# Decays over a whole tile of 128 positions, mirrored features folded in one step, and another order of attention, transpose and background steps

## The chip, the core and the metric

One NeuronCore of a Trainium2 chip runs the whole program. The metric is the time of one execution on the device, in microseconds (us); the median of three runs of the kernel before is 634.03 us (633.94 to 634.5). The change is small against that, so a verdict needs several runs of both kernels.

## What is computed

```python
# gated linear attention, batch 4, 8 heads, 768 positions, head size 48
for t in range(S):
    state = alpha[:, :, t, :, None] * state + einsum('bhd,bhe->bhde', k[:, :, t], v[:, :, t])
    y[:, :, t] = einsum('bhd,bhde->bhe', q[:, :, t], state)
x = y with the heads side by side            # (4, 768, 384)
u = x + real(fft(fft(x, axis=1), axis=2))    # over positions, then over features
un = (u - mean(u)) / sqrt(var(u) + 1e-6)
x2 = u + relu(un @ w_ch1) @ w_ch2            # 384 -> 1536 -> 384
out = (sigmoid(conv5(x2)) * (x2 @ w_val)) @ w_out
```

## The kernel before, in words

All matmuls are in fp32 or in pairs of fp32r halves (three matmuls stand for one product). The work is cut in three ways: the attention runs over tiles of 128 positions (6 tiles for each of the 4 batches, numbered g), the Fourier part over a batch, and the rest (norm, 384 to 1536 to 384, gate) over pieces of 256 positions, 12 in all. The weights arrive as 64-bit floats, and VectorE makes fp32 of them with three instructions of bit operations for each block of 384 columns (L222, L225, L229; `weight_parts`, and `convert_one` later on), ScalarE makes the high half (L233) and the low half comes from TensorE and ScalarE (L242 to L244) or from VectorE (L238).

**One attention tile** has four steps. `attn_a` makes running products of the decays with two scans (L288 from behind, L295 from the front, each restarted at a segment's end by a column of `ends` or `starts`), and multiplies k and q with them (L293, L298). Segments are 64 positions long, so a tile has two chunks and its scans have 8 segments of 65 columns. `attn_b` transposes k (L310), copies it (L311), and makes the scores chunk by chunk (L318), which VectorE masks (L319). `attn_c` makes the chunks' outer products of k and v (L335) and then steps the state twice: `sp` = state times the chunk's decay (L346), state = product + `sp` (L351). `attn_d` puts the scores times v (L366) and q times `sp` (L372) together, and copies the result to `x` with three ScalarE copies (L377 to L379) and one column by GpSimd (L380): features 1 to 255, feature 0 again, and the features from 383 down to 256, so that each feature and its mirror image (d and 384 - d) stand in two runs that are walked in step.

**The Fourier part** of a batch transposes `x` (`turn`, L472), adds and subtracts tiles t and t + 3 (L483, L484 in `fold`), and then adds and subtracts each feature and its mirror image: for each of two halves and two signs one instruction over 128 columns (L490) and one over 64 that reads backwards (L491), so eight for each of three t. GpSimd copies one column (L488). Matmuls follow (L514, L559), and the sums go into `u` (L564 to L583).

**The order of the work** is written by hand. Up to the first piece a list of strings, `FIRST`, gives it letter by letter: A, B, D the attention's steps, U and S the two parts of `attn_c`, w a part of a weight conversion, l weight loads, a, v, q loads of one tile, 0 to 2 `turn`, f, g, h `fold`, p and r matmuls of the Fourier part. From then on `run` walks through the matmuls of a piece (`mlp`, 24 parts); after each part it advances the norm of the next piece and the gate of the last one (`side`), the weight conversions, and a background generator that does attention and Fourier part of the next batch (`attention` by the string `ORDER`, in which a dot ends a part). How many background parts come after a part of `mlp` follows from `PACE`. The norm makes its reciprocal root on GpSimd (L630 to L636), writes it to DRAM (L640) and loads it back as rows (L644); `LAG_US`, `LAG_SS` and `LAG_RS` say how many parts it waits between its steps. All loads and stores go through SyncE's queue in program order; among them is the convolution's small weight table, `cw`, converted like the others.

In the text below S(b, i) is the state step (L346 and L351) of tile i of batch b, S(i) that of batch 0, and A, B, D, U likewise.

Of the kernel before, what the change touches and what calls it, by code (L numbers as in the profile page):

```python
# [33 lines left out]
CHECK_STEP = 5  # L34
# [15 lines left out]
W_DFT = (2, 1, 1, 0, 0, 0, 0, 0, 0, 1, 0)  # L50
# [10 lines left out]
A_W = 1 + 8 * (C + 1)  # L61
# [3 lines left out]
class Main:  # L65
# [21 lines left out]
    def constants(self):  # L87
# [11 lines left out]
        nc.vector.memset(self.ends.rearrange("p (g s) -> p g s", s=C + 1)[:, :, C : C + 1], 1.0)  # L99
# [176 lines left out]
    def attn_a(self, g):  # L276
# [189 lines left out]
    def turn(self, b, t):  # L466

        nc = self.nc
        for i in (t, t + 3):
# [701 lines left out]
```

## Time and profile before

The profiled execution took 632.62 us; its span, from the first to the last instruction, is 630.5 us. Times below are from the span's start.

| engine | busy us | share of the span | instructions |
|---|---|---|---|
| PE (matmul) | 584.1 | 93% | 6636 |
| PEld (weight load) | 547.1 | 87% | 6636 |
| DVE (VectorE) | 427.8 | 68% | 953 |
| ACT (ScalarE) | 242.7 | 38% | 577 |
| POOL (GpSimd) | 155.3 | 25% | 331 |

PE is near its limit over the span, but a mean says nothing of where the rest lies: the first matmul of the first piece (L651) stands at 88.09 us, and the stretches before and shortly after it look different from the rest.

### The profile page before, as it was taken

The page shows a single profiled execution, that of the slowest core. Times are in us where ns is not written, and L with a number is a line of the kernel's source. Part 1 is how long each engine was busy: PE and PEld are TensorE (multiplying, and loading weights), DVE is VectorE, ACT ScalarE, POOL GpSimd, SP SyncE. Part 2 cuts the span into 40 slices and gives each one's busy share as a digit, 9 for nine tenths or more (in the row PEclk, how much of TensorE's full clock was granted, in tenths as well). Part 3 has the DMA queues.
Part 4 walks back from the last instruction along what each step waited for, and adds up shares of the span by engine and source line. Part 5 has one row for each costly group of instructions (what it writes and reads, how often), then busy time and mean ns, then how long its engine had stood idle before and what let it go on. Part 6 is the DMA issues. An engine that isn't in the chain of part 4 may idle for free.

```text
span 630.5 us, 15960 instructions
## 1 busy us (share of the span) xinstructions
PE 584.1 (93%) x6636; PEld 547.1 (87%) x6636; DVE 427.8 (68%) x953; ACT 242.7 (38%) x577; POOL 155.3 (25%) x331
## 2 busy tenths in 40 slices
PE   3768899697999999999999999999999999999996
PEld 2546768686998899989999899899999999999995
DVE  7988779899926567966673858967763726363634
ACT  2333442224454355344453343353453344423222
POOL 0000215104125122133131144232312222322230
PEclk9868998789899999999999999999999999999998
DMA  9746352646232446633424433642431023110001
GB/s 350 276 139 232 110 175 10 190 151 153 73 119 74 101 133 147 152 115 91 122 78 98 124 107 73 196 132 85 115 107 37 26 80 82 52 10 26 9 3 55
DMA packets 29602, 69.50 MB, mean 110 GB/s; under 512 B 5200, under 2 KB 15952, under 8 KB 29520
## 3 DMA queue, kind: packets, MB, share of 16 engines
q1 hardware_dynamic: 29520, 68.38, 37.1%
q8 instruction: 54, 0.88, 0.6%
q14 instruction: 28, 0.23, 0.1%
HBM read 63.64 MB, written 4.73 MB: 108 GB/s over the span
## 4 chain that ended last, share of the span: by engine, by line
PE 70%; DVE 19%; DMA 4%; POOL 2%; issue 2%; ACT 2%; SPq 1%; DVEq 0%; POOLq 0%
PE ch L651 7%; PE mm L651 7%; PE ch L653 7%; PE ch L652 7%; PE mm L653 6%; PE mm L652 6%; PE aux L762 5%; PE aux L514 4%; PE aux L559 3%; PE aux L318 3%; DVE w L295 2%; DVE w L288 2%; PE aux L651 2%; PE aux L653 2%; PE aux L652 2%
## 5 line engine op out<-in xcount | busy, mean ns | idle before, releaser
L651 PE MATMUL ch<-hh,w2h 128*128 128x256 f32 x432 | 130.2, 301 | 0.2 <-ACT hh L672 0.2
L651 PE MATMUL mm<-hl,w1h 128*128 128x256 f32 x432 | 129.0, 298 | 1.0 <-ACT hl L608 1.0
L653 PE MATMUL ch<-hlo,w2h 128*128 128x256 f32 x432 | 122.9, 285 | 1.5 <-DVE hlo L674 1.5
L652 PE MATMUL ch<-hh,w2l 128*128 128x256 f32 x432 | 122.8, 284 | 0.0
L653 PE MATMUL mm<-hl,w1h 128*128 128x256 f32 x432 | 121.9, 282 | 0.0
L652 PE MATMUL mm<-hl,w1l 128*128 128x256 f32 x432 | 121.8, 282 | 0.0
L674 DVE SCALAR_TENSOR_TENSOR hlo<-mm,hh 128x512 fp32r<-128x512 f32 x72 | 49.5, 688 | 85.8 <-ACT hh L672 85.7
L651 PEld LDWEIGHTS mm<-hl,w1h 128*128 128x128 f32 x432 | 82.3, 190 | 4.0 <-ACT hl L608 1.4
L651 PEld LDWEIGHTS ch<-hh,w2h 128*128 128x128 f32 x432 | 82.5, 191 | 2.7 <-ACT hh L672 0.4
L653 PEld LDWEIGHTS ch<-hlo,w2h 128*128 128x128 f32 x432 | 82.8, 192 | 1.9 <-DVE hlo L674 1.9
L652 PEld LDWEIGHTS ch<-hh,w2l 128*128 128x128 f32 x432 | 82.7, 192 | 0.8
L652 PEld LDWEIGHTS mm<-hl,w1l 128*128 128x128 f32 x432 | 82.4, 191 | 0.8
L653 PEld LDWEIGHTS mm<-hl,w1h 128*128 128x128 f32 x432 | 82.4, 191 | 0.3 <-DVE hl L611 0.3
L672 ACT ACTIVATE hh<-mm 128x512 fp32r<-128x512 f32 x72 | 42.6, 591 | 59.7 <-PE mm L653 59.5
L726 DVE SCALAR_TENSOR_TENSOR ga<-u,cw,ga 128x256 f32<-128x256 f32 x132 | 58.0, 501 | 0.0
L748 POOL TENSOR_TENSOR hl<-ga,hl 128x256 fp32r<-128x256 f32 x33 | 25.6, 780 | 96.5 <-ACT hl L747 96.5
L617 POOL TENSOR_TENSOR tmp<-tmp,tmp 128x256 f32<-128x256 f32 x24 | 20.3, 847 | 100.6 <-ACT tmp L616 99.7
L380 POOL COPY x<-x 128x1 f32<-128x1 f32 x24 | 12.9, 535 | 123.3 <-ACT x L377 123.3
L318 PEld LDWEIGHTS aux<-w 48*64 48x64 f32 x768 | 27.5, 149 | 16.1 <-issue 8.2
L318 PE MATMUL aux<-w 48*64 48x64 f32 x768 | 30.8, 236 | 11.1 <-DVE w L298 6.0
L762 PE MATMUL aux<-wvo,hl 128*128 128x384 f32 x180 | 34.9, 337 | 0.0
L607 DVE TENSOR_TENSOR w<-u,aux 128x256 f32<-128x256 f32 x36 | 13.0, 417 | 28.2 <-PE aux L601 27.5
(182 smaller groups left out, 1184.2 us busy)
## 6 DMA issues: line engine op xcount, KB each, us to landing
qka<-in_qka_dram SPq DMA_DIRECT2D x23, 772.5 KB, 5.2
ck<-in_w_dram SPq DMA_DIRECT2D x24, 384.0 KB, 3.4
vu<-in_vu_dram SPq DMA_DIRECT2D x24, 192.0 KB, 3.6
u<-in_w_dram SPq DMA_DIRECT2D x12, 384.0 KB, 6.1
va<-in_va_dram SPq DMA_DIRECT2D x24, 192.0 KB, 4.0
ck<-in_al_dram SPq DMA_DIRECT2D x12, 384.0 KB, 3.4
out_dram<-ga SPq DMA_DIRECT2D x22, 192.0 KB, 1.9
w<-in_cs_dram SPq DMA_DIRECT2D x6, 579.0 KB, 5.2
```

The lines of the kernel that those rows point to most:

```text
L318: nc.tensor.matmul(out=sc[j * 64 : j * 64 + 64, cs], lhsT=kt[hs, cs], rhs=qt[hs, cs], start=True, stop=True)
L514: self.nc.tensor.matmul(out=pa[: d1 - d0, g * 193 : g * 193 + n], lhsT=self.eo[g][:, t, m, d0:d1], rhs=self.cs[g][:, t, m, :n], start=t == ...
L559: nc.tensor.matmul(out=pa[:, :385], lhsT=self.cd[:w, dt, mi, kt * P : (kt + 1) * P], rhs=pq[:w, mi, dt, :], start=dt == 0, stop=dt == 1)
L617: nc.gpsimd.tensor_tensor(out=ss, in0=ss, in1=sq, op=ALU.add)
L651: nc.tensor.matmul(out=out, lhsT=w[0][:, k, cols], rhs=xh, start=first, stop=False)
L652: nc.tensor.matmul(out=out, lhsT=w[1][:, k, cols], rhs=xh, start=False, stop=False)
L653: nc.tensor.matmul(out=out, lhsT=w[0][:, k, cols], rhs=xl, start=False, stop=last)
L672: nc.scalar.activation(out=hh, in_=hp, func=AF.Relu)
L674: nc.vector.scalar_tensor_tensor(out=hl, in0=hp, scalar=0.0, in1=hh.bitcast(F32), op0=ALU.max, op1=ALU.subtract)
L726: nc.vector.scalar_tensor_tensor(out=gs[:, j], in0=xs, scalar=w, in1=gs[:, j], op0=ALU.mult, op1=ALU.add)
L748: nc.gpsimd.tensor_tensor(out=gl[:, j], in0=gs[:, j], in1=gh[:, j].bitcast(F32), op=ALU.subtract)
L762: nc.tensor.matmul(out=po[:, :DM], lhsT=lh[:, k, ts], rhs=rh[:, k, :], start=n == 0, stop=n == 8)
```

## The change

Segments of the scans are now a whole tile: 4 segments of 129 columns. The decay of the second chunk is then part of q and k already, so the state is multiplied once for a tile: `s0` = state times the tile's decay, `s1` = `s0` + first product, state = `s1` + second product. For the first tile of a batch it is a copy and an addition, for the last one a multiplication and an addition. `x` is 386 columns wide; a feature and its mirror image now stand side by side, so `attn_d` writes it with two ScalarE copies that leave every second column out, and `fold` needs one instruction over 191 columns for each half and sign, which reads every second column twice. `turn` transposes columns 2, 4, ..., then 258 to 385, then 3, 5, .... The bound below which a decay sends the program to its general path goes from 0.5 to 0.6. `FIRST`, `ORDER`, `PACE` and `W_DFT` are other tables, `LAG_US` and `LAG_SS` go from 6 to 5, `CHECK_STEP` from 5 to 6.

```diff
-LAG_US = 6
-LAG_SS = 6
+LAG_US = 5
+LAG_SS = 5
-ORDER = "Bb.Aa..Dt.m.Cvc.q."
+ORDER = ".BAab..Dt..mCvc.q."
...
-A_W = 1 + 8 * (C + 1)
+A_W = 1 + NP * (P + 1)
...
@@ attn_c
-        pe = r["pend"].rearrange("p (a c) -> p a c", c=2)
         r["sp"] = self.t([P, 2, NP, D], "sp", 2)
-        for c in range(2):
-            if g % NT == 0 and c == 0:
-                st = self.t([P, NP, D], "st", 2)
-                nc.vector.tensor_copy(out=st, in_=ub[c])
-            else:
-                sp = r["sp"][:, c]
-                nc.vector.tensor_tensor(out=sp, in0=self.state,
-                                        in1=pe[:, :, c : c + 1].to_broadcast([P, NP, D]), op=ALU.mult)
-                if last and c == 1:
-                    break
-                st = self.t([P, NP, D], "st", 2)
-                nc.vector.tensor_tensor(out=st, in0=ub[c], in1=sp, op=ALU.add)
-            self.state = st
+        s0, s1 = r["sp"][:, 0], r["sp"][:, 1]
+        if g % NT == 0:
+            nc.vector.tensor_copy(out=s1, in_=ub[0])
+        else:
+            nc.vector.tensor_tensor(out=s0, in0=self.state, in1=r["pend"].unsqueeze(2).to_broadcast([P, NP, D]),
+                                    op=ALU.mult)
+            nc.vector.tensor_tensor(out=s1, in0=ub[0], in1=s0, op=ALU.add)
+        if not last:
+            self.state = self.t([P, NP, D], "st", 2)
+            nc.vector.tensor_tensor(out=self.state, in0=ub[1], in1=s1, op=ALU.add)
@@ attn_d
-        nc.scalar.activation(out=xt[:, :n], in_=yp[0][:, :n], func=AF.Copy)
-        nc.scalar.activation(out=xt[:, n:256], in_=yp[1][:, : 256 - n], func=AF.Copy)
-        nc.scalar.activation(out=xt[:, 257:385], in_=yp[1][:, n - 1 : 255 - n : -1], func=AF.Copy)
-        nc.gpsimd.tensor_copy(out=xt[:, 256:257], in_=xt[:, 0:1])
+        nc.scalar.activation(out=xt[:, 0:DM:2], in_=yp[0][:, :n], func=AF.Copy)
+        nc.scalar.activation(out=xt[:, DM + 1 : 1 : -2], in_=yp[1][:, :n], func=AF.Copy)
+        nc.gpsimd.tensor_copy(out=xt[:, 1 : DM + 1 : DM - 1], in_=xt[:, 0:1].to_broadcast([P, 2]))
@@ turn
-            for j in range(KD):
-                nc.tensor.transpose(pa[:, j * P : (j + 1) * P], self.x[:, i, j * P + 1 : (j + 1) * P + 1], self.ident)
+            x = self.x[:, i]
+            for j, xj in enumerate((x[:, 2:258:2], x[:, 258:], x[:, 3:258:2])):
+                nc.tensor.transpose(pa[:, j * P : (j + 1) * P], xj, self.ident)
@@ fold
-            nc.gpsimd.tensor_copy(out=e[:, 0, 0:1], in_=f[:, 0:1])
+            nc.gpsimd.tensor_copy(out=e[:, 0, ::192], in_=f[:, :: DM + 1])
             for m, o2 in ((0, ALU.add), (1, ALU.subtract)):
-                nc.vector.tensor_tensor(out=e[:, m, 1:129], in0=f[:, 1:129], in1=f[:, 257:385], op=o2)
-                nc.vector.tensor_tensor(out=e[:, m, 129:193], in0=f[:, 129:193], in1=f[:, 255:191:-1], op=o2)
+                nc.vector.tensor_tensor(out=e[:, m, 1:192], in0=f[:, 2:DM:2], in1=f[:, 3:DM:2], op=o2)
...
```

Three places show how instructions move. The first is VectorE between the scans of tile 3 and tile 4 of batch 0, with S(2) among them (`hl_61` and `hl_59` are the same conversion of two weight blocks, `qka` a tile's inputs). Before:

```order
L295 SCALAR_TENSOR_TENSOR w_377<-qka_199,starts 128x520
L298 TENSOR_TENSOR w_378<-qka_199,w_377 128x512
L222 TENSOR_SCALAR hl_61_386<-u_103 128x384 x2
L225 SCALAR_TENSOR_TENSOR hl_61_386<-u_103,hl_61_386 128x384 x2
L229 SCALAR_TENSOR_TENSOR hl_61_386<-u_103,hl_61_386 128x384 x2
L346 TENSOR_TENSOR sp_459<-st_322,pend_278 128x192
L351 TENSOR_TENSOR st_461<-mm_439,sp_459 128x192
L346 TENSOR_TENSOR sp_459<-st_461,pend_278 128x192
L351 TENSOR_TENSOR st_464<-mm_440,sp_459 128x192
L288 SCALAR_TENSOR_TENSOR w_468<-qka_313,ends 128x520
```

With the change:

```order
L295 SCALAR_TENSOR_TENSOR w_364<-qka_205,starts 128x516
L298 TENSOR_TENSOR w_365<-qka_205,w_364 128x512
L222 TENSOR_SCALAR hl_59_381<-u_103 128x384 x2
L225 SCALAR_TENSOR_TENSOR hl_59_381<-u_103,hl_59_381 128x384 x2
L343 TENSOR_TENSOR sp_449<-st_326,pend_250 128x192
L345 TENSOR_TENSOR sp_449<-mm_429,sp_449 128x192
L348 TENSOR_TENSOR st_452<-mm_430,sp_449 128x192
L229 SCALAR_TENSOR_TENSOR hl_59_381<-u_103,hl_59_381 128x384 x2
L288 SCALAR_TENSOR_TENSOR w_460<-qka_321,ends 128x516
```

The state step has three instructions for four, and the conversion's last pair (L229) now stands behind it.

The second place is SyncE's queue around the loads for tile 4 of batch 0 (`vu`, `va` are the tile's v for U and for D, `wvo<-in_cs` the two Fourier tables, the others weight blocks). Before:

```order
L273 DMA va_577<-in_va_dram 128x384
L268 DMA vu_579<-in_vu_dram 128x384
L500 DMA wvo_581<-in_cs_dram 128x1158 x2
L199 DMA hl_102_623<-in_w_dram 128x768
L199 DMA u_103<-in_w_dram 128x768
L273 DMA va_689<-in_va_dram 128x384
```

With the change:

```order
L273 DMA va_543<-in_va_dram 128x384
L495 DMA wvo_573<-in_cs_dram 128x1158 x2
L268 DMA vu_576<-in_vu_dram 128x384
L199 DMA hl_98_612<-in_w_dram 128x768
L199 DMA u_103<-in_w_dram 128x768
L273 DMA va_679<-in_va_dram 128x384
```

The Fourier tables have gone ahead of tile 4's `vu`; its `va` still stands behind two weight blocks.

The third place is VectorE in the first piece, where the norm's two small instructions (L625 and L626, now L620 and L621) start the reciprocal root. Before:

```order
L674 SCALAR_TENSOR_TENSOR hlo_1101<-mm_1073,hh_1099 128x512
L222 TENSOR_SCALAR hl_179_1114<-w_1055 128x384
L225 SCALAR_TENSOR_TENSOR hl_179_1114<-w_1055,hl_179_1114 128x384
L229 SCALAR_TENSOR_TENSOR hl_179_1114<-w_1055,hl_179_1114 128x384
L238 TENSOR_TENSOR w1l<-hl_173_1083,w1h 128x384
L625 TENSOR_SCALAR nv_1132<-aux_1129 128x2
L626 TENSOR_SCALAR ny_1133<-nv_1132 128x2
L222 TENSOR_SCALAR hl_185_1161<-u_103 128x384
```

With the change:

```order
L669 SCALAR_TENSOR_TENSOR hlo_1071<-mm_1043,hh_1069 128x512
L620 TENSOR_SCALAR nv_1087<-aux_1084 128x2
L621 TENSOR_SCALAR ny_1088<-nv_1087 128x2
L222 TENSOR_SCALAR hl_177_1092<-w_1025 128x384
L225 SCALAR_TENSOR_TENSOR hl_177_1092<-w_1025,hl_177_1092 128x384
L229 SCALAR_TENSOR_TENSOR hl_177_1092<-w_1025,hl_177_1092 128x384
L238 TENSOR_TENSOR w1l<-hl_167_1053,w1h 128x384
L222 TENSOR_SCALAR hl_179_1131<-u_103 128x384
```

The two now stand ahead of a conversion of four instructions that stood ahead of them.

## Rows read from the trace of the kernel before

**Rows 1.** Busy time by stretch: window, its length, each engine's busy us, PE clock, DMA.

```profile
0.00:88.00 88.00, 62.87 (x896) 48.85 (x896) 69.62 (x161) 30.21 (x80) 6.24 (x20) 0.88 0.61 212
88.00:160.00 72.00, 60.09 (x776) 55.39 (x777) 65.64 (x130) 21.55 (x55) 18.87 (x38) 0.86 0.50 136
...
200.00:605.00 405.00, 402.08 (x4303) 385.88 (x4302) 258.58 (x578) 164.19 (x384) 114.81 (x238) 1.00 0.33 90
```

**Rows 2.** Chain that ended last, 84 to 204 us: start, length, what.

```profile
111.40 6.50 DMA u<-in_cw_dram
...
156.66 0.61 DVE w L298
...
157.41 1.97 PE aux L318 x32
...
159.89 0.21 PE mm L652
...
165.13 0.12 PE ch L652
...
171.22 1.08 PE aux L318 x32
```

**Rows 3.** VectorE in order of time around S(1): start, length, what, idle before.

```profile
25.63 1.02 DVE L229 SCALAR_TENSOR_TENSOR hl<-hl,hl 128x384 int32<-128x384 int32 x2
26.57 0.36 DVE L346 TENSOR_TENSOR sp<-st,pend 128x192 f32<-128x192 f32 x1
27.03 0.36 DVE L351 TENSOR_TENSOR st<-mm,sp 128x192 f32<-128x192 f32 x1
27.42 0.36 DVE L346 TENSOR_TENSOR sp<-st,pend 128x192 f32<-128x192 f32 x1
...
28.92 0.69 DVE L319 TENSOR_TENSOR w<-aux,mask 128x512 f32<-128x512 f32 x1 [0.68 <-PE aux L318]
```

**Rows 4.** VectorE in order of time, start of S(2) and second instruction of S(3).

```profile
38.18 0.35 DVE L346 TENSOR_TENSOR sp<-st,pend 128x192 f32<-128x192 f32 x1
...
47.69 0.36 DVE L351 TENSOR_TENSOR st<-mm,sp 128x192 f32<-128x192 f32 x1 [3.14 <-PE mm L335]
```

**Rows 5.** SyncE's queue in order of time: issue, length, what.

```profile
48.10 1.99 SPq L500 DMA_DIRECT2D wvo<-in_cs_dram  x2
...
51.33 0.60 SPq L273 DMA_DIRECT2D va<-in_va_dram  x1
```

**Rows 6.** TensorE in order of time, start of D(4).

```profile
57.47 1.11 PE L366 MATMUL aux<-va,w 64*64 64x48 f32 x29 [0.84 <-DMA va<-in_va_dram]
```

**Rows 7.** VectorE in order of time, first `fold` of batch 0 and the second's start.

```profile
62.46 0.56 DVE L483 TENSOR_TENSOR f<-x 128x385 f32<-128x385 f32 x1
...
63.60 0.29 DVE L490 TENSOR_TENSOR w<-f 128x128 f32<-128x128 f32 x1
63.80 0.22 DVE L491 TENSOR_TENSOR w<-f 128x64 f32<-128x64 f32 x1
...
64.95 0.56 DVE L483 TENSOR_TENSOR f<-x 128x385 f32<-128x385 f32 x1
```

**Rows 8.** GpSimd in order of time, the edge column of tile 5.

```profile
67.05 1.99 POOL L380 COPY x<-x 128x1 f32<-128x1 f32 x1 [3.12 <-ACT x L377]
```

**Rows 9.** VectorE in order of time, first piece.

```profile
96.48 0.35 DVE L222 TENSOR_SCALAR hl<-w 128x384 int32<-128x384 int32 x1
...
98.40 0.15 DVE L625 TENSOR_SCALAR nv<-aux 128x2 f32<-128x2 f32 x1
...
117.92 0.17 DVE L222 TENSOR_SCALAR u<-u 128x15 int32<-128x15 int32 x1 [2.55 <-DMA u<-in_cw_dram]
```

**Rows 10.** Groups by line and shape: count, busy us, mean ns, idle before, releaser.

```profile
L674 DVE SCALAR_TENSOR_TENSOR hlo<-mm,hh 128x512 fp32r<-128x512 f32 x72 | 49.5, 688 | 85.8 <-ACT hh L672 85.7
...
L472 PEld LDWEIGHTS aux<-ident,x 128*128 128x128 f32 x72 | 8.7, 148 | 2.4 <-POOL x L380 1.9 <-ACT x L377 0.2
...
L623 PEld LDWEIGHTS aux<-avg,tmp 128*128 128x128 f32 x48 | 6.6, 195 | 1.3 <-issue 1.3
```

More of the change, by code (lines that the diff above doesn't have):

```diff
@@ L33 @@
 CHECK_FROM = 1
-CHECK_STEP = 5
+CHECK_STEP = 6
 W_SCALE = 2.0**20
@@ L49 @@
 N_NORM = 10
-W_DFT = (2, 1, 1, 0, 0, 0, 0, 0, 0, 1, 0)
+W_DFT = (2, 0, 2, 0, 0, 0, 0, 0, 0, 1, 0)
 W_CAP = 2
@@ L98, in constants @@
         nc.vector.memset(self.ends, 0.0)
-        nc.vector.memset(self.ends.rearrange("p (g s) -> p g s", s=C + 1)[:, :, C : C + 1], 1.0)
+        nc.vector.memset(self.ends.rearrange("p (g s) -> p g s", s=P + 1)[:, :, P : P + 1], 1.0)
         self.starts = cp.tile([P, A_W - 1], F32, name="starts")
@@ L280, in attn_a @@
         al = qka[:, :A_W]
-        k = qka[:, A_W : A_W + 512].rearrange("p (g s) -> p g s", s=C)
-        q = qka[:, A_W + 512 :].rearrange("p (g s) -> p g s", s=C)
+        k = qka[:, A_W : A_W + 512].rearrange("p (g s) -> p g s", s=P)
+        q = qka[:, A_W + 512 :].rearrange("p (g s) -> p g s", s=P)
         sp = self.t([P, 2, A_W - 1], "w", 5)
         sfx, pre = sp[:, 0, :], sp[:, 1, :]
-        sfx3, pre3 = (x.rearrange("p (g s) -> p g s", s=C + 1) for x in (sfx, pre))
+        sfx3, pre3 = (x.rearrange("p (g s) -> p g s", s=P + 1) for x in (sfx, pre))
         qk = self.t([P, 2, 512], "w", 5)
@@ L289, in attn_a @@
                                      initial=0.0, op0=ALU.mult, op1=ALU.add)
-        pend = self.t([P, 8], "pend", 3)
+        pend = self.t([P, NP], "pend", 3)
         nc.scalar.activation(out=pend, in_=sfx3[:, :, 0], func=AF.Copy)
-        nc.vector.reciprocal(out=self.starts.rearrange("p (g s) -> p g s", s=C + 1)[:, :, 0], in_=sfx3[:, :, 0])
-        nc.vector.tensor_tensor(out=kt.rearrange("p (g s) -> p g s", s=C), in0=k, in1=sfx3[:, :, 1:], op=ALU.mult)
+        nc.vector.reciprocal(out=self.starts.rearrange("p (g s) -> p g s", s=P + 1)[:, :, 0], in_=sfx3[:, :, 0])
+        nc.vector.tensor_tensor(out=kt.rearrange("p (g s) -> p g s", s=P), in0=k, in1=sfx3[:, :, 1:], op=ALU.mult)
         yield
@@ L297, in attn_a @@
         yield
-        nc.vector.tensor_tensor(out=qt.rearrange("p (g s) -> p g s", s=C), in0=q, in1=pre3[:, :, 1:], op=ALU.mult)
+        nc.vector.tensor_tensor(out=qt.rearrange("p (g s) -> p g s", s=P), in0=q, in1=pre3[:, :, 1:], op=ALU.mult)
         self.at[g] = dict(qt=qt, kt=kt, pend=pend)
@@ L510, in dft_term @@
     def dft_term(self, pa, m, dt, t):
-        d0, d1 = ((0, 97), (97, 193))[dt] if m == 0 else ((1, 97), (97, 193))[dt]
+        d0, d1 = ((0, 97), (97, 193))[dt] if m == 0 else ((1, 97), (97, 192))[dt]
         for g in range(2):
@@ L557, in dft @@
                 for dt in range(2):
-                    w = 97 if (mi == 0 and dt == 0) else 96
+                    w = (97, 96, 96, 95)[2 * mi + dt]
                     nc.tensor.matmul(out=pa[:, :385], lhsT=self.cd[:w, dt, mi, kt * P : (kt + 1) * P],
@@ L983, in scanned @@
             al, k, q, z = (self.t([P, NT, P], n, 1) for n in ("al", "k", "q", "z"))
-            for dst, o in ((k, A_W), (q, A_W + 512)):
+            for dst, o in ((al, 1 + pr), (k, A_W), (q, A_W + 512)):
                 o += pr * P
                 nc.sync.dma_start(out=dst, in_=self.ap["qka"][g, :, o : o + P].rearrange("g p s -> p g s"))
-            for t in range(NT):
-                for c in range(2):
-                    o = 1 + (2 * pr + c) * (C + 1)
-                    nc.sync.dma_start(out=al[:, t, c * C : (c + 1) * C], in_=self.ap["qka"][b * NT + t, :, o : o + C])
             ys = [self.t([P, NT // 2, 2, D], f"ys{i}", 1, pool=self.ps) for i in range(2)]
@@ L1061, in general @@
         xp = ctx.enter_context(self.tc.tile_pool(name="xp", bufs=1))
-        self.x = xp.tile([P, NT, DM + 1], F32, name="general_x")
+        self.x = xp.tile([P, NT, DM + 2], F32, name="general_x")
         self.heads = xp.tile([P, 2], F32, name="heads")
```

35 lines of the change are left out of this document (18 added, 17 removed).

## The prediction

> **What bounds the kernel now.** I read the busy time by stretch first, since PE's 93% is a mean. From 200 to 605 us PE is busy 402.1 of 405 us at full clock, and VectorE 258.6 [rows 1]: less work for VectorE is worth nothing there. Up to 88 us it is the other way round: PE stands idle 25.1 us, and VectorE is busy 69.6. From 88 to 160 us PE is idle 11.9 us of 72 and VectorE 6.4 [rows 1]. So only the first 160 us can answer, some 37 us of PE's idle time. The chain of waits agrees: from the small table `cw`, whose load is 6.5 us on the chain, it runs through VectorE to L298 at 156.66 and only then back to PE [rows 2]. VectorE's own order of time shows what is in the way: state steps in a row, moved conversions, and a few waits [rows 3, 4, 9].
>
> **The state step.** S has three instructions for four. One costs 0.46 us from its start to the next one's when that needs its result, 0.39 when it need not [rows 3]. The first and last tile of a batch lose one too.
>
> **The head, to 69 us.** S(0) and S(1) lie on VectorE's path: 0.92 us. The pair L229 that stood ahead of S(2) goes behind it; such a pair takes 0.94 us [rows 3]. The mask of tile 2 waited 0.68 us for its scores [rows 3]; on PE they stood behind U(1) and a conversion that waited for U(1)'s load, and U(1) now comes behind that conversion, so I count this wait as gone. S(2) starts 0.92 + 0.94 + 0.68 = 2.54 us earlier than 38.18 [rows 4]. Then PE sets the pace: D(2), B(3), a conversion and U(3) follow each other, and S(3) waits 3.14 us for U(3) [rows 4]. D(2)'s second half needed S(2)'s third instruction and now needs its second, 0.39 us less. U(3) comes 2.93 us earlier, at 44.8. The pair moved behind S(2) falls into the 3.14 us wait: VectorE gets there 2.54 + 0.46 - 0.94 = 2.06 us earlier, so 2.3 us of wait are left to hide it. If that cover went, the pair would cost its 0.94 again. S(3) and S(4) give 0.92 more, 3.85 in all by S(5).
>
> What is late next is U(5), which stands behind D(4) on PE, and D(4) waits for its `va`, issued at 51.33, needed at 57.47 [rows 5, 6]. The two tables whose issue took 1.99 us go ahead and no longer delay it; but D(3), which frees the buffer, now stands behind U(4). I put the issue at 49.8, an estimate: 2.93 us earlier by U(3), less 1.4 for U(4) and its load. With the old 6.1 us from issue to use, D(4) comes 1.6 us earlier; with a load that no longer shares the queues with the tables, S(5) keeps the whole 3.85.
>
> `fold` then has four instructions of 191 columns for eight. The step from L490 to L491 is 0.20 us, and the eight take 64.95 - 63.60 = 1.35 [rows 7], so L491 steps by 0.14: 64 columns make 0.06, and one of 191 makes 0.20 + 0.06 = 0.26. That is 1.35 - 1.06 = 0.28 for a fold (rounded), 0.55 for the two that VectorE does before the Fourier matmuls; the third lies beside them. The Trainium skill has another rule (VectorE: DVE Perf Modes, The DRAIN you can't avoid): the next operation does not start until the pipeline is empty. By it a fold would save 4 x (0.29 + 0.22) - 4 x 0.36 = 0.60 us, and the sum would be 0.6 us lower. The row shows L491 starting 0.09 us before L490 ends, so it speaks against the rule here, and I use the steps; 626.6 by the rule gets 0.02 of the forecast's chance.
>
> These columns are read with a stride of two. L229 reads every second word too, and takes 0.47 us for 384 columns [rows 3], 1.22 ns a column; L298 reads none so and takes 0.61 for 512 [rows 2], 1.19. I cost the stride at nothing; if two strided inputs cost double (0.19 us more for each of the eight instructions), the two folds lose 1.0 us instead of gaining 0.55.
>
> Behind the folds, GpSimd's column copy for tile 5 took 1.99 us, to 69.04 [rows 8], though it moves one column; VectorE was busy without a pause until then, and the transposes wait for the copy. I read from this that the copy ends with VectorE's run, so the folds' 0.55 us counts; if it ends when D(5) allows, the 0.55 is lost.
>
> Head: between 1.6 + 0.55 = 2.2 (rounded) and 3.85 + 0.39 (S(5)) + 0.55 = 4.8 us. I take **3.5**, the middle. From 69 to 88 us PE does the same matmuls one behind the other: nothing.
>
> **The first pieces, 88 to 160 us.** The norm's two instructions go ahead of a conversion that takes 98.40 - 96.48 = 1.92 us [rows 9]. On them hang the reciprocal root on GpSimd, its trip through DRAM, and behind that, on SyncE's queue, the load of `cw`, issued at 111.40 [rows 2]; VectorE waits 2.55 us for it at 117.92 [rows 9]. VectorE gets there when it did, as the conversion only changes place. The wait falls to 0.63: **1.9 us** (bounds 0, if something else on the queue is late, and 2.55). From there to 156.66 the chain is VectorE [rows 2], with S(1,0), S(1,1) and S(1,2) in it: 3 x 0.46 = **1.4 us**.
>
> **Everything later: 0.** The state steps, folds and ScalarE copies of batches 1 to 3 that remain lie beside a full PE. `turn` loads 48 of its 72 stationary blocks with a stride of two. A strided load elsewhere (L623) takes 195 ns, the transposes' own 148 [rows 10]; 36 blocks beside a full PE x 0.047 bound this at 1.7 us. I take 0, as TensorE's loads overlap its matmuls.
>
> **Sum.** 3.5 + 1.9 + 1.4 = 6.8 us. The profiled execution of 632.62 us becomes 625.8; it lies 1.41 below the median of 634.03, so I predict **627.2**. A measurement of this kernel can tell about 0.2%, 1.3 us, from no change.
>
> **Rivals.**
> - *Only the removed instructions count.* The waits for `va` and `cw` stay as they are, and what was moved runs into them. Then S(0) and S(1) 0.92, folds 0.55 and 1.4 in the first pieces: 2.9 us, 631.1. For it: D(3)'s new place and a queue in program order. Against it: the 1.92 us by which the norm starts earlier has nothing else in its way that the rows show.
> - *The clock gives more.* Behind the last long pause PE ran at the lower level of 1.2 GHz: L318 took 1.97 us where it takes 1.08, and the next 16 or so matmuls 0.21 where they take 0.12 [rows 2]. If shorter pauses keep the clock at 2.4 GHz there, 0.89 + 16 x 0.09 = 2.3 us come on top: 624.9. Against it: the pause gets shorter, but stays.
> - *The new order costs PE.* `ORDER` puts the mask behind the two scans in one part, so VectorE works on one part 0.69 us longer [rows 3]. If the split of the hidden layer (L674), for which PE waits, comes that much later once in each of the 18 tiles of batches 1 to 3, that is 12.4 us: 634.03 - 6.8 + 12.4 = 639.6, slower. It decides where VectorE has less than 0.69 us to spare in front of L674. On the mean it has 85.8 / 72 = 1.2 us, waiting for ScalarE [rows 10]; so I give it little.
> - *Nothing comes of it*: the late `va`, strided folds and strided loads together take up what is saved, 634.
>
> **How the numbers follow.** Forecast 0.58, clock 0.13, only instructions 0.15, slower by the order 0.07, nothing 0.07. The first three are faster by more than 0.2%: 0.86; same 0.07; slower 0.07. The range goes from the clock's case with a head of 4.8 us and the bound of `cw` (623.0) to the case of only the instructions and 0.9 us above it (632.0), which leaves out the slower case and nothing, 0.14, and the far ends.
>
> **What would show it.** Right: the first matmul of the first piece 3 to 4 us before 88.09; VectorE's wait for `cw` under 1 us; S steps of three instructions; copies and folds no longer in duration for their columns; PE's idle time from 200 us on unchanged. Wrong: D(4) still near 57, a wait for `cw` above 2 us, or waits of PE for L674 or for scores after 200 us, which would make the order the cause.

## The result and the profile after

The change takes 626.19 us (median of 4 runs, 625.43 to 627.54), the kernel before 633.99 (4 runs); the ratio is 0.9894, with a 95% interval of 0.9865 to 0.9924. 627.2 was predicted, faster by more than 0.2%. The profiled execution took 625.92 us, 6.7 less than that of before; its span is 624.1 us, 6.4 less.

Busy time by stretch, with cuts at the same places of the program (columns as in [rows 1]):

```profile
0.00:84.00 84.00, 63.46 (x900) 49.29 (x901) 67.48 (x146) 30.96 (x77) 5.48 (x20) 0.90 0.65 227
84.00:153.00 69.00, 61.26 (x864) 56.62 (x862) 65.26 (x130) 21.06 (x50) 21.16 (x38) 0.93 0.50 139
153.00:193.00 40.00, 37.15 (x443) 35.59 (x444) 19.45 (x46) 18.66 (x40) 16.45 (x37) 0.96 0.28 78
193.00:598.50 405.50, 402.97 (x4294) 388.12 (x4293) 245.98 (x533) 165.45 (x374) 111.88 (x234) 1.00 0.34 91
```

PE is idle 20.5 us up to 84 us where it was 25.1, and 7.7 us in the next stretch where it was 11.9 [rows 1]. VectorE's busy time from 193 us on is 246.0 us for 258.6, and PE is as full there as before.

The start of the first matmul of the first piece, TensorE in order of time:

```profile
83.12 0.38 PE L646 MATMUL mm<-hl,w1h 128*128 128x256 f32 x1 [0.96 <-ACT hl L603]
```

It stood at 88.09. Further on, the same instruction of both kernels can be set side by side. I take ScalarE's copy of the hidden layer (`hh<-mm`, 72 in a run) and write how much earlier than in the first trace of before it starts. A single value can be off by a microsecond where background work stands a little ahead or behind; the columns matter by their trend. The lower lines are the experiments below; before_again is a second trace of the kernel before.

| kernel | copy at 109.90 before | at 197.95 | at 300.33 | at 608.93 |
|---|---|---|---|---|
| the change | 5.01 | 8.73 | 8.29 | 6.50 |
| tables_only | 2.00 | 5.95 | 4.96 | 5.37 |
| edits_only | 2.15 | 3.63 | 4.16 | 1.99 |
| order_back | 6.19 | 10.37 | 11.00 | 9.74 |
| pad64 | 4.79 | 8.65 | 7.18 | 8.41 |
| both_back | 4.54 | 9.53 | 10.44 | 12.44 |
| start_0_32 | 3.59 | 8.90 | 10.15 | 14.27 |
| lag6 | 3.40 | 6.64 | 7.80 | 5.92 |
| state_only | 3.05 | 6.20 | 6.62 | 7.14 |
| fold_only | -0.64 | 1.52 | 2.00 | 2.38 |
| before_again | -1.37 | 0.80 | 0.74 | 0.75 |

So the change was 8.7 us ahead of the first trace of before by 198 us (7.9 of the second), more than the 6.8 of my sum, and lost 2.2 us again where I had counted nothing. Total right, terms not: this is what the experiments had to explain.

### The profile page after: what moved, and what is told of

It reads as the page before. It is cut to its first block, busy times and chain, and to the rows that moved or that the text cites. A ratio compares the mean times of both kernels' runs of the same rounds, so it can differ in the third digit from the quotient of the medians.

```text
span 624.1 us, 15821 instructions
## 1 busy us (share of the span) xinstructions
PE 584.7 (94%) x6636; PEld 548.7 (88%) x6636; DVE 409.9 (66%) x881; ACT 241.9 (39%) x553; POOL 156.3 (25%) x331
## 4 chain that ended last, share of the span: by engine, by line
PE 74%; DVE 16%; DMA 3%; POOL 2%; ACT 2%; issue 2%; SPq 0%; DVEq 0%; POOLq 0%; ACTq 0%
PE mm L646 7%; PE ch L646 7%; PE ch L647 7%; PE mm L647 7%; PE ch L648 7%; PE mm L648 7%; PE aux L757 5%; PE aux L509 4%; PE aux L554 3%; PE aux L318 2%; DVE w L295 2%; DVE w L288 2%; PE aux L646 2%; PE aux L647 2%; PE aux L648 2%
## 5 line engine op out<-in xcount | busy, mean ns | idle before, releaser
L646 PE MATMUL mm<-hl,w1h 128*128 128x256 f32 x432 | 129.6, 300 | 1.0 <-ACT hl L603 1.0
L646 PE MATMUL ch<-hh,w2h 128*128 128x256 f32 x432 | 129.7, 300 | 0.2 <-ACT hh L667 0.2
L648 PE MATMUL ch<-hlo,w2h 128*128 128x256 f32 x432 | 122.3, 283 | 1.5 <-DVE hlo L669 1.5
L648 PE MATMUL mm<-hl,w1h 128*128 128x256 f32 x432 | 123.3, 285 | 0.0
L647 PE MATMUL mm<-hl,w1l 128*128 128x256 f32 x432 | 123.2, 285 | 0.0
L669 DVE SCALAR_TENSOR_TENSOR hlo<-mm,hh 128x512 fp32r<-128x512 f32 x72 | 49.6, 689 | 100.7 <-ACT hh L667 100.4
L646 PEld LDWEIGHTS mm<-hl,w1h 128*128 128x128 f32 x432 | 83.3, 193 | 4.0 <-ACT hl L603 1.4
L646 PEld LDWEIGHTS ch<-hh,w2h 128*128 128x128 f32 x432 | 82.3, 190 | 2.8 <-ACT hh L667 0.4
L648 PEld LDWEIGHTS mm<-hl,w1h 128*128 128x128 f32 x432 | 83.7, 194 | 0.3 <-DVE hl L606 0.3
L648 PEld LDWEIGHTS ch<-hlo,w2h 128*128 128x128 f32 x432 | 81.5, 189 | 1.9 <-DVE hlo L669 1.9
L721 DVE SCALAR_TENSOR_TENSOR ga<-u,cw,ga 128x256 f32<-128x256 f32 x132 | 54.9, 476 | 0.0
L375 POOL COPY x<-x 128x2 f32<-128x2 f32 x24 | 12.6, 527 | 137.2 <-ACT x L374 137.2
L612 POOL TENSOR_TENSOR tmp<-tmp,tmp 128x256 f32<-128x256 f32 x24 | 18.1, 755 | 72.2 <-ACT tmp L611 71.3
L318 PEld LDWEIGHTS aux<-w 48*64 48x64 f32 x768 | 26.2, 144 | 9.9 <-issue 4.0
L727 POOL TENSOR_TENSOR hl<-u,hl 128x768 fp32r<-128x768 f32 x11 | 20.2, 1840 | 45.0 <-ACT hl L712 41.8
```

The lines of the kernel that those rows point to most:

```text
L318: nc.tensor.matmul(out=sc[j * 64 : j * 64 + 64, cs], lhsT=kt[hs, cs], rhs=qt[hs, cs], start=True, stop=True)
L646: nc.tensor.matmul(out=out, lhsT=w[0][:, k, cols], rhs=xh, start=first, stop=False)
L647: nc.tensor.matmul(out=out, lhsT=w[1][:, k, cols], rhs=xh, start=False, stop=False)
L648: nc.tensor.matmul(out=out, lhsT=w[0][:, k, cols], rhs=xl, start=False, stop=last)
L669: nc.vector.scalar_tensor_tensor(out=hl, in0=hp, scalar=0.0, in1=hh.bitcast(F32), op0=ALU.max, op1=ALU.subtract)
L721: nc.vector.scalar_tensor_tensor(out=gs[:, j], in0=xs, scalar=w, in1=gs[:, j], op0=ALU.mult, op1=ALU.add)
```

## Experiments

All medians, and the ratio to the kernel before on the same chip:

| run | median us | before | ratio, 95% interval |
|---|---|---|---|
| tables_only | 628.19 | 632.46 | 0.9929 (0.9905 to 0.9953) |
| edits_only | 630.46 | 632.46 | 0.9979 (0.9959 to 1.0) |
| order_back | 623.1 | 632.46 | 0.9877 (0.9847 to 0.9908) |
| pad64 | 622.74 | 632.46 | 0.9857 (0.9827 to 0.9886) |
| both_back | 619.84 | 631.22 | 0.9814 (0.9783 to 0.9845) |
| shift32 | 620.01 | 631.22 | 0.9818 (0.9784 to 0.9851) |
| shift96 | 620.33 | 631.22 | 0.9819 (0.9785 to 0.9852) |
| lag6 | 625.18 | 632.47 | 0.9894 (0.9848 to 0.994) |
| state_only | 628.47 | 632.47 | 0.9946 (0.9916 to 0.9976) |
| fold_only | 630.12 | 632.47 | 0.9965 (0.9947 to 0.9983) |
| start_0_32 | 617.6 | 631.62 | 0.9777 (0.9749 to 0.9804) |

**Order alone, instructions alone.** tables_only is the kernel before with FIRST, ORDER, PACE, W_DFT, the lags and CHECK_STEP of the change; edits_only the change with those of before. The first as a diff to the kernel before (the second is its reverse, from the change):

```diff
-LAG_US = 6
-LAG_SS = 6
+LAG_US = 5
+LAG_SS = 5
-FIRST = ("Alwwlqwwl", "BlaAlUwqwSvl", "lBDAwwllUaqvlSw", "BwlwwAwDallwUvSq", "AllylDBwUSavx", "BwAlDUSlawwv", "BawDlU0lSww1lfl", "lDg2wpllrh")
+FIRST = ("lAwlwwlql", "llBwwlaAUSvqwll", "BwAwDwlUaqSvll", "BlwwAlwwallDUvSq", "wAylDlBwaUSwxv", "BAllUSlDlwawv", "BawDllU0lSww1lfl", "lDg2wlllplhrl")
-ORDER = "Bb.Aa..Dt.m.Cvc.q."
+ORDER = ".BAab..Dt..mCvc.q."
...
```

> The kernel before with all the tables and lags of the change (FIRST, ORDER, PACE, W_DFT, LAG_US, LAG_SS, CHECK_STEP), its own instructions. Theory 1, order and instructions add up: of the 7.8 us that the change gained, my sum put 2.9 on removed instructions (S 0.92, folds 0.55, first pieces 1.4) and the rest on order, so 634.0 - 4.9 = 629.1, the wait for cw is gone, and the first matmul of the first piece stands about 3 us before 88.09. Theory 2, the order only pays because the steps got shorter: 633 to 635, the first matmul within 1 us of 88.09.

> The changed kernel with all tables and lags of the kernel before: only the instructions are changed. Theory 1 (they add up): 634.0 - 2.9 = 631.1, the wait for cw still about 2.5 us, first matmul of the first piece 1.5 us before 88.09. Theory 2 (shorter chain from D(5) to the transposes and a higher clock there come from the instructions: the short column copy 1.7, the clock 1.5): 634.0 - 2.9 - 3.2 = 627.9, first matmul near 83.5 to 84, PE at full clock between U(5) and the transposes.

By their ratios the order alone gains 0.71%, 4.5 us (4.9 forecast), the instructions alone 0.21%, 1.3 us (2.9 forecast). The first matmul of the first piece is at 85.95 and 85.97, 2.1 us earlier in each, 4.3 of the change's 5.0. That the two add up in the head is only as good as single traces are: the eight traces below with the change's FIRST and instructions have this matmul at 81.94 to 84.72, the two of before at 88.09 and 89.45. edits_only drifts: 2.2 us of its lead are gone between 300 and 609 us, with the tables of before, while tables_only keeps its own. Something in the instructions makes a full PE slower.

**Where the buffers stand.** In the trace of the change the matmuls of 256 columns that stream a part of `hl` (L646 to L648, `mm`) follow each other by 119.4 ns on the mean, in that of before by 117.4 (from one start to the next, the step; the mean is of all under 145 ns, over 1,100 in each trace). The segments of 129 columns make each of the two `qka` buffers 32 bytes shorter; all later buffers move 64 or 32 bytes down. pad64 undoes this for `hl` (`hh` and `hlo` end 32 bytes past their old place):

```diff
-        qka = self.t([P, QKA_W], "qka", 2)
+        qka = self.t([P, QKA_W + 8], "qka", 2)[:, :QKA_W]
```

> The changed kernel with each of the two qka buffers 32 bytes wider, which puts all later buffers but hh, hlo, f, ga where they stood before (64 bytes further); nothing else. In the trace of the change the matmuls of 256 columns that read uh and ul (L646 to L648, mm) step by 119.4 ns, before by 117.4, all at full clock, some 3 us over the run. Theory 1, the place of the operand in memory: the steps return to 117.4, total 626.2 - 3 = 623. Theory 2, the chips differ and not the program: steps the same as in the other kernels of this call, with or without the changed layout, total 626.

pad64 takes 622.74 us, and the step is 117.7 ns, while order_back and edits_only, on the same chip with the buffers of the change, have 119.4. So it is the place, not the chip. By the ratios the pad gains 0.37%, 2.3 us, with intervals that overlap; its steps are worth twice that (1.7 ns for 1,296 matmuls here, 1.9 for as many `ch`, the second group of the table further on). From 110 to 300 us PE stands idle 2.0 us longer in pad64 than in the change, which takes up part of it; from 300 to 609 us, where PE is full in both, pad64 is 3.0 us faster. TensorE in order of time, matmuls of the first piece, the change:

```profile
84.25 0.28 PE L646 MATMUL mm<-hl,w1h 128*128 128x256 f32 x1
...
86.77 0.28 PE L646 MATMUL mm<-hl,w1h 128*128 128x256 f32 x1
```

The same of pad64, and below it of start_0_32:

```profile
84.82 0.28 PE L646 MATMUL mm<-hl,w1h 128*128 128x256 f32 x1
...
87.30 0.28 PE L646 MATMUL mm<-hl,w1h 128*128 128x256 f32 x1
```

```profile
85.30 0.28 PE L646 MATMUL mm<-hl,w1h 128*128 128x256 f32 x1
...
87.75 0.28 PE L646 MATMUL mm<-hl,w1h 128*128 128x256 f32 x1
```

21 steps each: 2.52, 2.48 and 2.45 us, 120.0, 118.1 and 116.7 ns. The durations (0.28 everywhere) say nothing; the starts do.

**ORDER and PACE.** order_back takes only these two from the kernel before, both_back also pads `qka` as above.

```diff
-ORDER = ".BAab..Dt..mCvc.q."
-PACE = (1, 0.8, 0.95, 1.15, 0.85, 0.65, 0.95, 1.1, 1.2, 1, 1, 1)
+ORDER = "Bb.Aa..Dt.m.Cvc.q."
+PACE = (1, 0.8, 0.95, 1.15, 0.85, 0.85, 0.95, 0.95, 1, 1, 1, 1)
```

> The changed kernel with ORDER and PACE of the kernel before; FIRST, W_DFT and lags stay. If the waits of PE for a buffer read by ScalarE (L373, 2.4 us) and for va (1.9 us) between 153 and 193 us come from the new ORDER: they go, PE's idle time there falls from 2.85 to under 1 us and the total to about 624.2. If they come from the instructions or from an earlier start of the stage: they stay, 626 to 627. If the new ORDER also saved VectorE time earlier: slower than 626.2, 627 to 629. The head up to the first piece is the same, 83.1.

> The changed kernel with ORDER and PACE of the kernel before and each qka buffer 32 bytes wider (hl buffers start 32 bytes past a multiple of 128, hh and hlo at a multiple). If the two effects are independent (ORDER and PACE 1.5 to 2 us between 84 and 300 us, the place of the buffers 2 us over the run), their ratios add: to the kernel before 0.9877 with the order alone, 0.9840 here, some 2 us under order_back; the step of the 256-column matmuls is 117.5 ns and PE idle from 191 us on about 0.5 us. If the place of the buffers only moved the waits in pad64, it stays at 0.9877.

The waits of PE from the first piece to about 600 us, the change (engine, line, what it waited for, us in total, times, longest):

```profile
PE aux L362 <- DMA va<-in_va_dram: 3.6, 2, 1.9
PE aux L335 <- ACT x L373: 3.3, 2, 2.4
PE aux L318 <- DVE w L602: 2.0, 1, 2.0
PE ch L648 <- DVE hlo L669: 1.5, 2, 1.3
...
PE aux L318 <- DVE w L298: 0.6, 1, 0.6
```

The same of order_back:

```profile
PE aux L318 <- DVE w L298: 3.4, 1, 3.4
PE aux L318 <- DVE w L602: 3.1, 1, 3.1
PE ch L648 <- DVE hlo L669: 1.5, 2, 1.3
PE aux L310 <- ACT x L373: 1.2, 2, 0.7
...
PE aux L335 <- ACT x L373: 0.9, 1, 0.9
```

With the new ORDER and PACE the waits for VectorE are shorter (L602 and L298, 6.5 to 2.6 us), but others stand in their place: 3.6 us for `va`, whose load now comes one part later, and 3.3 for a buffer. ScalarE in order of time shows the second, in the change:

```profile
154.70 0.21 ACT L291 ACTIVATE pend<-w 128x4 f32<-128x4 f32 x1 [6.84 <-DVE w L288]
154.82 0.33 ACT L373 ACTIVATE x<-aux 128x192 f32<-128x192 f32 x1
```

and TensorE:

```profile
150.61 0.68 PE L368 MATMUL aux<-sp,w 64*64 64x48 f32 x32
...
155.20 1.03 PE L335 MATMUL aux<-vu,w 64*64 64x48 f32 x30 [2.41 <-ACT x L373]
...
156.97 0.41 PE L646 MATMUL mm<-hl,w1h 128*128 128x256 f32 x1
157.18 0.41 PE L647 MATMUL mm<-hl,w1l 128*128 128x256 f32 x1
```

D's matmuls were done at 151.3, but ScalarE's copy of them stood behind the small copy `pend`, which waited 6.84 us for a scan on VectorE; U (L335) needed the buffer. Behind the pause the matmuls step by 0.21 us for a while where they take 0.12 (granted clock 0.89 from 150 to 165 us). In order_back `pend` waits too, 3.1 us, but PE does not wait there; it has waited 3.4 us for L298 a little before. The medians put order_back 0.17% below the change and both_back 0.43% below pad64, each with intervals that overlap; the offsets (10.37 to 8.73 at 198 us) have part of their lead from the head, where the two are the same program. Pairs with the same buffers compare best: from 110 to 300 us order_back gains 4.8 us and the change 3.3, both_back 5.9 and pad64 2.4. So in these traces the new ORDER and PACE cost 1.5 to 3.5 us; the medians alone do not show a cost. With the pad on top of order_back, both_back is at 0.9814 (0.984 expected), and the interval of the change lies wholly above its own: together the two steps back are faster than the change.

**What in a buffer's place matters.** shift32 widens `vu` instead of `qka`, shift96 both, each on order_back. start_0_32 is shift32 with 64 bytes more in front of the `hh` buffers, which is this:

```diff
-        v = self.t([P, 2, NP, D], "vu", 1)
+        v = self.t([P, 2 * NP * D + 8], "vu", 1)[:, : 2 * NP * D].rearrange("p (j a d) -> p j a d", j=2, a=NP)
...
-        f = self.t([P, DM + 2], "f", 1)
+        f = self.t([P, DM + 18], "f", 1)[:, : DM + 2]
```

> The changed kernel with ORDER and PACE of the kernel before and the vu buffer 32 bytes wider instead: hl starts at a multiple of 128 bytes, hh and hlo 96 past one. Theory 1, only the first 64 bytes of a 128-byte stretch are a good start: uh and ul as moving operand (mm) step by 117.5 ns, hh and hlo (ch) by over 118.3, total within 1 us of both_back. Theory 2, any start that is no multiple of 64 costs, and zero is best: mm 117.0 or less. Theory 3, it was the particular address and not its remainder: 119.4, total 2 us above both_back.

> The changed kernel with ORDER and PACE of the kernel before, qka buffers and vu each 32 bytes wider: hl starts 64 past a multiple of 128 bytes, hh and hlo 32 past one. Theory 1 (second half of 128 bytes is the bad start): mm 119.4 ns, ch 117.6, total between order_back and both_back. Theory 2 (multiples of 64 are good): mm 117.5 and total as both_back. Theory 3 (particular address): cannot say.

> As shift32 with the buffer f 64 bytes wider: hl starts at a multiple of 128 bytes, hh and hlo 32 past one. So far, moving operands of 256 columns stepped by 117.2 ns (hl at 0), 117.6 (32), 119.6 (64), 119.5 (96); hh and hlo by 117.9 (0), 116.0 (32), 119.6 (64), 118.5 (96). If the start alone decides: mm 117.2, ch 116.0, which takes 1296 x 2.5 ns = 3.3 us from shift32: 616.7, ratio to before 0.977, PE idle unchanged. If waits take up what PE saves, as they did for half in pad64: 618.5.

Mean step by where the moving operand (the one that streams through TensorE) starts past a multiple of 128 bytes, from all kernels that have it there; the starts are the addresses that the built programs give the buffers:

| start | `hl` (L646 to L648, `mm`) | `hh`, `hlo` (`ch`) |
|---|---|---|
| 0 | 117.0 to 117.1 ns | 117.8 to 117.9 |
| 32 | 117.4 to 117.7 | 115.7 to 115.9 |
| 64 | 119.6 | 119.7 |
| 96 | 119.4 | 118.5 to 118.6 |

A start in the second 64 bytes is slower, by 0.6 to 4 ns of 118, in both groups. The change has 96 and 64, so it pays in both groups. Every pad moves other buffers too, so that the operand's own start is what counts is read from the agreement of the two groups; and it is not the whole rule, since 0 is better than 32 for `hl` and worse for `hh`. My first expectation for shift32 and shift96 held for the steps of `mm`; that 32 would be best for `hh` by 2 ns I had not seen, and it is why shift96 is no slower than both_back. start_0_32 came out at 617.6 (616.7 expected): it is faster than the change (0.9894) by more than both intervals. With 2.0 ns for 1,296 matmuls `mm` and 1.1 for 1,296 `ch`, the change pays about 4 us for this against the kernel before. Why the memory answers so, no run shows.

**The lags.** lag6 is the change with the old lags.

```diff
-LAG_US = 5
-LAG_SS = 5
+LAG_US = 6
+LAG_SS = 6
```

> The changed kernel with LAG_US and LAG_SS back at 6. Theory 1, the lags took the wait for cw away: VectorE waits 2 to 2.7 us at cw again, the kernel is that much slower up to 190 us, 628 to 629 in all (0.993 of before). Theory 2, FIRST did it (other weight blocks left to convert): no wait for cw, 626.

Neither theory: a wait of 0.41 us, and the time of the change. It also bears on ORDER: with the new ORDER and PACE but the old lags PE does not wait for `va` at all, where the change waits 3.6 us and pad64 3.5, and from 110 to 300 us lag6 gains 4.4 us, nearly as much as order_back. The waits for `va` thus need the new lags as well, while the wait for the buffer that ScalarE reads (L335) stays, 2.8 us. Its load of `cw` is issued 22.8 us behind the first matmul of the first piece, in the change 21.05 (104.17 - 83.12): the lags do move it, 1.75 us. But the wait of 2.55 us [rows 9] was not the order's. before_again is the kernel before, unchanged, for a second trace.

> The kernel before, unchanged, for a second trace of it. The load of cw took 6.5 us in the first trace and in edits_only 6.1, in all others 4.5 to 5.1. Theory 1, the wait of 2.55 us for cw belongs to the order of the kernel before: again 2.2 to 2.6. Theory 2, it belongs to the one execution: the load takes about 4.8 us and the wait is 0.4 to 0.8, as in lag6, state_only and fold_only, which issue it as late. First matmul of the first piece: 88.1 if the head is steady, 86.5 to 88.7 if it varies as between the kernels that share the new FIRST (81.94 to 84.72).

VectorE in order of time, where [rows 9] has its third line, in that second trace of before:

```profile
117.62 0.17 DVE L222 TENSOR_SCALAR u<-u 128x15 int32<-128x15 int32 x1 [0.88 <-DMA u<-in_cw_dram]
```

and in the change:

```profile
109.65 0.67 DVE L319 TENSOR_TENSOR w<-aux,mask 128x512 f32<-128x512 f32 x1
110.23 0.17 DVE L222 TENSOR_SCALAR u<-u 128x15 int32<-128x15 int32 x1
```

The load took 6.5 us in the first trace, 5.2 in the second, 6.1 in edits_only and 4.5 to 5.1 in all others. With the old lags the wait was therefore 0.4 to 2.55 us, with the new ones it was nothing in any trace.

**One edit at a time.** state_only is the kernel before with segments of 128 positions and the state step in three instructions (`qka` padded); fold_only with the new layout of `x`, the two copies and the fold. Of the change's diff they take these places, with the layout of the inputs that belongs to each:

```diff
@@ state_only
-A_W = 1 + 8 * (C + 1)
+A_W = 1 + NP * (P + 1)
...
+            nc.vector.tensor_tensor(out=s1, in0=ub[0], in1=s0, op=ALU.add)
...
@@ fold_only
+        nc.scalar.activation(out=xt[:, 0:DM:2], in_=yp[0][:, :n], func=AF.Copy)
...
+                nc.vector.tensor_tensor(out=e[:, m, 1:192], in0=f[:, 2:DM:2], in1=f[:, 3:DM:2], op=o2)
```

> The kernel before, its tables and its fold, with segments of 128 positions and the state step in three instructions (buffers where they stood, by the wider qka). By my sum S(0) and S(1) give 0.92 us in the head, more if S(3) and S(4) count, and 1.4 us between 113 and 155 us: 634.0 - 2.3 = 631.7, first matmul of the first piece at 87.2, wait for cw still 2.5 us. If the gain of the instructions in the head is all in the column copy and the folds: first matmul unchanged, only 1.4 to 1.7 us, 632.5.

> The kernel before with mirrored features side by side, two strided copies and the fold in four instructions, everything else as before. By my sum the two folds give 0.55 us and the rest nothing: 633.5. By the traces of the runs so far, from the end of D(5) on ScalarE to the first Fourier matmul it is 0.8 us with these instructions and 2.3 without, and D(5) does not come earlier: 1.5 us, first matmul of the first piece at 86.5, total 632.5. If the strided loads of the transposes cost the 36 x 0.037 us by which they are longer: 1.3 of that is given back after 200 us.

628.47 and 630.12 us: 0.5% and 0.35%, each more than expected. state_only is 3.05 us ahead in the head in its trace, which is its fastest run (625.31), and keeps 7.14; fold_only is behind before's first trace in the head and 0.7 ahead of the second. Its `hh` and `hlo` start at a multiple of 128 bytes, those of before 96 past one; by its steps of `mm` and `ch` some 0.6 us of its gain is the place of the buffers. Its column in the table stays at 2.0 to 2.4 from 300 us on: the transposes' strided loads cost little behind full matmuls, though they take longer than the 148 ns of [rows 10]. From start to start the 36 transposes after 200 us take 3.67 us in fold_only and 3.44 in before. The group in the change:

```profile
L468 PEld LDWEIGHTS aux<-ident,x 128*128 128x128 f32 x72 | 9.5, 185 | 0.9 <-POOL x L375 0.7
```

Together the two gain 0.89%, while edits_only, which has both with the buffers of the change, gains 0.21%. The gap, 4.3 us, is near the 4 us that the place of the buffers was found to cost, though each of the three ratios is uncertain by 0.2 to 0.3%.

The scatter of the head has one visible cause. All engines in order of time around the column copy of tile 5, in order_back:

```profile
62.31 0.62 DVE L222 TENSOR_SCALAR hl<-u 128x384 int32<-128x384 int32 x2
...
62.48 0.23 POOL L375 COPY x<-x 128x2 f32<-128x2 f32 x1 [3.83 <-ACT x L374]
...
62.77 0.39 PE L468 MATMUL aux<-ident,x 128*128 128x128 f32 x1 [0.43 <-POOL x L375]
```

and in both_back, which has the same instructions there:

```profile
62.76 0.62 DVE L222 TENSOR_SCALAR hl<-u 128x384 int32<-128x384 int32 x2
...
62.93 1.44 POOL L375 COPY x<-x 128x2 f32<-128x2 f32 x1 [3.84 <-ACT x L374]
63.30 1.02 DVE L225 SCALAR_TENSOR_TENSOR hl<-u,hl 128x384 int32<-128x384 int32 x2
...
64.42 0.39 PE L468 MATMUL aux<-ident,x 128*128 128x128 f32 x1 [1.63 <-POOL x L375]
```

The copy either slips through in 0.23 us or ends 0.05 us behind VectorE's run (64.37 to 64.32), and PE's transposes wait for it, 1.63 us here. Of the eight traces with the change's FIRST and instructions it was long in three, with the first piece at 83.60 to 84.72, and short in five, at 81.94 to 83.41; in both traces of before and in tables_only it was long, 1.94 to 1.99 us, in state_only 0.18. The Trainium skill (SBUF — State Buffer, SBUF: two separate sides) says that GpSimd and VectorE share a pair of ports, that whichever instruction starts first gets it for the whole instruction, and that the other blocks fully; of VectorE it names instructions in a two-port mode or with two SBUF inputs. The traces agree that the copy waits for VectorE, but here it waited for a run of several instructions (the four of L222 and L225 in both_back).

## Why the prediction was right in total and wrong in its terms

**The head (3.5 forecast, bounds 2.2 to 4.8; 4.97 in the trace).** The term was mis-sized, and single traces split it only roughly: in the eight with the change's FIRST and instructions the first matmul stands 3.4 to 6.2 us before that of before's first trace. In the change's own trace the steps of attention up to S(5) came out near the lower bound; in the seven others they lie on both sides of the upper one. What follows D(5) the sum had wrong: a short column copy gave about 1.3 us in five of the eight, and the folds' 0.55 came in none.

- S(2) came 1.5 us earlier, not 2.54 [rows 4]. The mask of tile 2 no longer waits [rows 3], and the pair L229 gives its 0.94, but S(0) itself starts 0.29 us later, and its 0.46 went into a new wait of 0.59 us of tile 1's mask. VectorE in order of time, the change:

```profile
20.23 0.69 DVE L319 TENSOR_TENSOR w<-aux,mask 128x512 f32<-128x512 f32 x1 [0.59 <-PE aux L318]
...
36.70 0.35 DVE L343 TENSOR_TENSOR sp<-st,pend 128x192 f32<-128x192 f32 x1
...
46.20 0.36 DVE L345 TENSOR_TENSOR sp<-mm,sp 128x192 f32<-128x192 f32 x1 [2.62 <-PE mm L335]
```

- D(4) starts at 55.69, 1.8 us earlier [rows 6], inside my "at least 1.6". It no longer waits for `va`, but everything in front of it on PE is only that much earlier: S(5)'s last step gains 2.2 us, not 3.85. In the seven others D(4) starts at 52.37 to 53.99 and that step is 3.4 to 5.0 us earlier, on both sides of the 3.85.
- The folds cost what the steps said. The first takes 62.10 - 59.88 = 2.22 us for 2.49 [rows 7]: 0.27, forecast 0.28. The rule of the Trainium skill that I weighed (VectorE: DVE Perf Modes, The DRAIN you can't avoid) would have made it 0.60; the trace is against it. The same section adds that a next operation which is not held starts earlier, and the trace agrees with that: the second fold instruction starts 0.27 us behind the first, which takes 0.35. The stride is free here: two instructions of 191 columns take 0.62 us.

```profile
59.88 0.56 DVE L479 TENSOR_TENSOR f<-x 128x386 f32<-128x386 f32 x1
60.54 0.56 DVE L480 TENSOR_TENSOR x<-x 128x386 f32<-128x386 f32 x1
61.02 0.62 DVE L486 TENSOR_TENSOR w<-f 128x191 f32<-128x191 f32 x2
61.56 0.62 DVE L486 TENSOR_TENSOR w<-x 128x191 f32<-128x191 f32 x2
62.10 0.55 DVE L479 TENSOR_TENSOR f<-x 128x386 f32<-128x386 f32 x1
```

- The clock moved; that it gave anything is not shown. From U(5) to D(5) PE does the same matmuls. The stretch in the change, in lag6, which has the same instructions up to the first piece, and in the first trace of before (columns as in [rows 1]):

```profile
57.90:61.70 3.80, 3.74 (x34) 3.11 (x34) 3.47 (x10) 2.96 (x10) 1.02 (x3) 1.00 0.99 329
```

```profile
56.78:62.24 5.46, 5.46 (x34) 4.12 (x35) 4.35 (x12) 3.34 (x9) 1.01 (x3) 0.69 0.95 333
```

```profile
59.70:65.40 5.70, 5.68 (x34) 4.50 (x34) 4.91 (x17) 3.29 (x10) 1.03 (x3) 0.61 0.98 332
```

  3.8 us at a granted clock of 1.00 (2.4 GHz) for 5.7 at 0.61, much of it at 1.2 GHz: 1.9 us. But the change's trace stands alone. In lag6 and the six others with its FIRST and instructions the stretch takes 5.45 to 5.47 us at 0.69, hardly less than in before. There the clock was at 1.00 from 48.2 us to U(5). In the change's trace the low clock lay earlier, which cost time in front of U(5) instead:

```profile
48.20:53.20 5.00, 3.73 (x99) 3.37 (x99) 3.86 (x6) 0.78 (x3) 0.25 (x1) 0.66 0.64 189
```

  The clock fell shortly before 50 us, where PE had stood idle 1.3 of 1.8 us. It had comparable pauses in the others, so why it fell there in this trace alone stays open. U(5) starts at 57.96 in the change and at 55.19 to 56.78 in the seven, D(5) at 61.78 and at 60.65 to 62.24: what the clock gives back in this stretch it had taken ahead of it. So the 1.9 us is luck of one execution, and the rival "the clock gives more" is not borne out here, nor where I had put it: behind the pause at 155 us the matmuls still step by 0.21 us for a while.
- "The copy ends with VectorE's run, so the folds' 0.55 us counts" failed for the change. D(5)'s last ScalarE copy allows the column copy at 63.61 for 67.05 [rows 8], 3.44 us earlier, and it took 0.29 us for 1.99, so the Fourier matmuls start at 64.41 for 69.37, 4.96 earlier: 3.44 by D(5), 1.5 by the copy, nothing by the folds. GpSimd in order of time, the change:

```profile
63.61 0.29 POOL L375 COPY x<-x 128x2 f32<-128x2 f32 x1 [2.19 <-ACT x L374]
```

  The 1.5 is partly luck: with the long copy of both_back the first piece would have begun near 84.3.

**`cw` (1.9).** The step "the norm's two instructions go ahead, so the load is issued 1.92 us earlier" holds: relative to the first matmul it is 2.3 us earlier, 1.75 of it by the lags. What failed was to take the 2.55 us of one trace as the price: it hung on a load of 6.5 us that took 5.2 in another execution. Against the first trace it gave all of 2.55, against the second 0.88.

**The state steps behind it (1.4).** edits_only, whose wait for `cw` is nearly that of the first trace (2.24 us), is 2.17 us ahead at the hidden-layer copy that stood at 113.58 and 3.82 at the one that stood at 152.45: 1.65, or 1.3 without the 0.31 us by which its wait is shorter. The term is right.

**"Everything later: 0" failed**, by some 4 us of PE time for buffers that moved, and in the traces by the waits that the new ORDER and PACE brought (1.5 to 3.5 us from 110 to 300 us). Neither is a matter of covered work, which is how I had argued. Of the rival "the new order costs PE" the place was wrong: not L669 (1.5 us of waits in both) but U behind ScalarE's queue, and `va`; its effect is seen in the traces, and the medians leave it open. That this rival was not the outcome is due to the gain in front of it. A surplus of about 2 us before 198 us and a loss of 2.2 behind it met at the forecast: the total was right by luck.

## What to carry to other kernels

Set the same instruction of two traces side by side along the whole run: the lead at each stage shows gains and losses that a right total hides. Where PE is full, compare the starts of equal matmuls, since a buffer made 32 bytes shorter can move every operand behind it. And a wait for a transfer, or a stretch at another clock, in one trace is worth one execution: look at how long it took in other traces of the same instructions before it goes into a sum or an explanation.

## What was not expected of the hardware

- Matmuls of 256 columns step by 115.7 to 119.7 ns depending on where their moving operand starts within 128 bytes, at full clock, on several chips; a start in the second 64 bytes costs more. Padding alone took order_back from a ratio of 0.9877 (0.9847 to 0.9908) to 0.9777 (0.9749 to 0.9804) in start_0_32.
- GpSimd's copy of one or two columns took 0.18 to 1.99 us, by how it fell among VectorE's instructions.
- The same instructions up to the first piece found the low clock at different places: 0.66 from 48.2 to 53.2 us and 1.00 over the 34 matmuls between U(5) and D(5) in the change's trace, 1.00 and 0.69 in lag6 and the six others.
- The load of 15 KB for `cw` took 4.5 to 6.5 us from issue to landing. The kernel before ran from 627.83 to 634.79 us.
